# An LSH attention and token-mixing kernel on one core: idle-time matmuls at the start, new engines for the bit copies, and a new order of all steps

## The chip, the core and the metric

The kernel runs on one core of a Trainium2 chip. The core's engines work side by side, each through a queue of its own in program order: TensorE (PE, with its weight loads listed as PEld), VectorE (DVE), ScalarE (ACT), GpSimd (POOL) and SyncE (SP), which here issues nearly all DMAs. An engine waits at the head of its queue until semaphores of other engines or DMAs release it, and all that is queued behind waits too. The metric is the device time of one execution in microseconds (us); lower is better.

## The reference, cut to what matters

```python
batch, n_heads, seq, head_dim = 4, 8, 768, 64        # d_model 512, 6 projection bits
q_bits = (einsum('bhsd,dk->bhsk', q, proj) > 0)      # likewise k_bits
q_bucket = sum(q_bits * powers, axis=-1)             # likewise k_bucket
mask = q_bucket[:, :, :, None] == k_bucket[:, :, None, :]
scores = where(mask, matmul(q, k.T) / sqrt(64), -1e9)
attn = softmax(scores);  x = matmul(attn, v)         # heads side by side: (4, 768, 512)
theta = x @ w_theta
y = w_tok_r @ (x * cos(theta)) + w_tok_i @ (x * sin(theta))   # over the 768 tokens, per batch
u = x + y
out = u + maximum(u @ w_ch, 0)
```

## The kernel before, in words

Attention is done head by head in 16 pairs of heads (4 batches of 4 pairs; `prep_qk` and `prep_v` prepare a pair). Q and K are scaled by powers of two and split into a high and a low f16 half. The bucket test becomes part of the scores' matmul: the signs of the six projections of a pair are computed by `bits` (fp32 matmuls `pb`) and `sign` (DVE, L523, tile `rows`), and for each head its 24 rows of signs are copied below Q and K in the operand tile `qk` of that head. These copies are the operations `fbit` in `assemble`: four a head, each 24x384 f16, two for Q (a plain copy, on DVE or POOL at L588) and two for K (a multiplication by a column that is 1 in this head's rows and 0 in the others: on DVE or POOL at L586; on ACT both kinds stand at L584). The text calls the first plain copies and the second masking copies. There are three operand tiles, so a copy also waits until the last score matmul of the head that had the tile before. The first head of all has copies of its own (`piece`, lines 536 to 540).

A head then runs nine blocks of maxima (`qmax` on PE into tile `sq`, `vmax` on DVE, L632), which give a row bound that is written back into `qk` by a small DMA, then six or three score blocks per part (`st`), an exponential on ACT (`pf`, L713), its f16 rounding on ACT (`p1`, L719), the remainder on POOL (`p2`, L725) and the products with V on PE (`pv`, tile `po`). Ten heads of the later batches take another route (`bst`, `bmax` L836, `bpf` L864, `bp1` L872, `bp2` L878, `bpv`). When a batch's heads are done, `moe` runs the mixing for it: `proj` with w_theta (tile `ps_th`), sine and cosine, `zf`, `zh`, `zl` (L1109), 72 groups of three `y` matmuls (tile `py`), and `proj` with w_ch (tile `ps_r`), `relu`, `fin` and `store`. The weights are brought into f16 halves during the first batch (`wlow`, `whigh`, `wmul`, `wtl` on DVE, `wsign`, `wabs`, `wth` on ACT).

Nothing runs in the order in which it is written. The code first builds a list of 4263 operations. Each names one or more engines on which it may run with a planner's cost in ns, the operations it depends on and the buffers ("slots") that it holds. `issue_all` then issues them in the order of the string `ORDER`: each word is an engine letter (P, A, D, G for POOL, S) and the operation's number in base 36. The string `SLOTS` gives each slot the number of its buffer. Both strings were found by a search over the planner's costs outside the kernel; nothing of the search runs on the chip. PSUM has eight banks: two `mx`, two `s` and four `m`.

```python
own.append(op("fbit", prio + AB, {"POOL": (480, bits("POOL", i, x)), "DVE": (160, bits("DVE", i, x)),
                                  "ACT": (480, bits("ACT", i, x))}, t["bits"] + free_after, [sr]))
```

Of the kernel before, what the change touches and what calls it, by code (L numbers as in the profile page):

```python
# [32 lines left out]
def lsh_attention_moe_kernel(ctx: ExitStack, tc: tile.TileContext, q, k, v, proj, w_theta, w_tok_r, w_tok_i, w_ch, out):  # L33
# [6 lines left out]
    P = 128  # L40
# [524 lines left out]
    def assemble(j, n_, t, prio, free_after):  # L565
# [3 lines left out]
        sh, sr = t["slots"]  # L569
# [636 lines left out]
SETS = 3  # L1206
CL = 0.321
# [11 lines left out]
AB = 0.006  # L1219
# [47 lines left out]
    "0000000000000000000001010120112100212102100010000022001110100000011011011031022201000011221333111110000333122211110010310131201021"  # L1267
    "1001110310011130011111000200101101010210233013001322113302111000123303220111101030200110300130100013200002310011100013011110000100"
    "1120021011022213000211100011220311113312010121001100302011110320011110001100101301100100101111022312110300013313220011120013230132"
    "0001200120003110012000103000021010011100200110011100210311100020123211030311113213130201102000323130102201113101010320201131301201"  # L1270
    "1101200130000011010010011111110031131131232132003111032100302201131001212200010311221311120000321123020003111000000003210100001012"
    "0102320100123212131132001303320000102101031001201110010132101013231030110002221110330011310111111003103131000101130220023213200132"
    "0101031301101202111333103211110020100122012303100003000231010100110301301011213012012320223001003320301112311002301011111102002010"
    "3331031200002111110300013010111111012110231010113320010032311121231100003230112012011230101123310012000201111320200012100012001101"
    "0011201200111310323123101120000032300310112001013301030111013221102101032031111211110020010101011010012113230023101001323002301121"
    "2310100132300010223001230110331110103012012101200100010000121100001010201320101332010302111220101113030120003200111032100321012012"
    "0022301123030011310111300010111000011013102302120301201303023210111003022002321000032301020010113110232311003201322000010300001111"
    "0001111301211101031332002003031011012210030230101012000122321000131130220033110033101110330013211000101113100223101111220203103000"
    "1110111220003213113301013020122202001033013113100212000032112200321120001211211202212020200110110032200303112211020101310011320021"
    "1130002011320020201210021002311210002221120300123112020011001132002000221100113100301212012110211110030031010321012000022211110000"  # L1280
    "10112100021120000011021021012101021103200120001120000100120113002"
# [213 lines left out]
```

## Time and profile before

| | |
|---|---|
| time, median of 3 runs | 720.29 us (717.54 to 721.21) |
| the profiled execution | 716.42 us, of which the span from its first to its last instruction is 714.6 us |
| PE busy | 665.1 us (93% of the span) |
| ACT busy | 595.2 us (83%) |
| DVE busy | 586.0 us (82%) |
| POOL busy | 458.9 us (64%) |

The profile has one row a group of instructions: where it stands in the code, the tile written and read, the count, the busy time, the mean duration and the idle time of the engine just before it with what ended it. Matmuls are pipelined, so a mean duration of one holds the time in which it overlaps its neighbours; what a matmul costs in a stream is the distance from start to start. An fp32 matmul leaves two records.

### The profile page before, as it was taken

Reading aid. Unit: us, or ns where it says so; the run is one execution under the profiler, and the core shown is the slowest. Engines: PE = TensorE matmul, PEld = TensorE weight load, DVE = VectorE, ACT = ScalarE, POOL = GpSimd, SP = SyncE. Lnnn points to the kernel's source line nnn. Section 1 sums busy time; section 2 is a strip of 40 time slices with the busy share of each in tenths; the row PEclk is TensorE's granted clock in tenths of the full one; section 3 lists DMA queues with packets and bytes.
Section 4 is the critical chain, followed back from the end, with each engine's and each line's share of the span. In section 5 each row is a group of like instructions: output and inputs, shape, how many; then the busy total and the mean of one; then the engine's idle time right before and its main releaser. Section 6 shows DMA issues by size and latency. Waiting matters only on the chain.

```text
span 714.6 us, 16736 instructions
## 1 busy us (share of the span) xinstructions
PE 665.1 (93%) x6174; PEld 387.4 (54%) x6174; DVE 586.0 (82%) x1317; ACT 595.2 (83%) x1058; POOL 458.9 (64%) x448
## 2 busy tenths in 40 slices
PE   3788989989999999998999999999999999999997
PEld 1266657664555565555555566564545565654443
DVE  5899989999999899899998789878998766868221
ACT  6789989998999999999998898899898788876001
POOL 6566686868544787897847778886645878731011
PEclk9999999999999999999999999999999999999999
DMA  6748766666324557899864779797642866861112
GB/s 209 212 135 226 185 154 179 149 155 172 90 56 99 153 91 153 170 189 178 150 160 70 148 145 188 156 217 154 137 99 52 146 148 122 143 109 60 44 45 88
DMA packets 193304, 98.92 MB, mean 138 GB/s; under 512 B 166984, under 2 KB 182984, under 8 KB 193224
## 3 DMA queue, kind: packets, MB, share of 16 engines
q1 hardware_dynamic: 193080, 97.85, 62.2%
q8 instruction: 48, 0.79, 0.5%
q14 instruction: 32, 0.26, 0.1%
q10 hardware_dynamic: 144, 0.03, 0.0%
HBM read 32.53 MB, written 6.29 MB: 54 GB/s over the span
## 4 chain that ended last, share of the span: by engine, by line
PE 36%; DVE 18%; ACT 12%; issue 3%; ACTq 0%; DVEq 0%
PE py L77 16%; PE ps_r L77 6%; PE po L77 4%; PE st L77 3%; DVE bm L836 3%; ACT pf L864 3%; PE bt L77 3%; DVE mc L632 2%; PE ps_th L77 2%; PE sq L77 2%; ACT late L872 1%; ACT pf L713 1%; ACT p L719 1%; DVE f L1098 1%; DVE s_x L980 1%
## 5 line engine op out<-in xcount | busy, mean ns | idle before, releaser
L725 POOL TENSOR_TENSOR p<-pf,p 128x512 f16<-128x512 f32 x162 | 202.5, 1261 | 82.8 <-ACT p L719 60.1
L77 PE MATMUL py<-z,wtk 128*128 128x512 f16 x864 | 205.0, 379 | 1.2 <-DVE z L1109 0.8
L878 POOL TENSOR_TENSOR late<-pf,late 128x384 f16<-128x384 f32 x120 | 117.7, 993 | 52.4 <-ACT late L872 45.3
L77 PEld LDWEIGHTS <-qk 120*128 120x128 f16 (+2 forms) x1032 | 96.4, 101 | 96.8 <-issue 38.8
L632 DVE TENSOR_REDUCE mc<-sq 128x1 f32<-128x512 f32 (+1 forms) x198 | 131.1, 683 | 15.4 <-PE sq L77 14.2
L77 PEld LDWEIGHTS <-wtk 128*128 128x128 f16 x864 | 82.3, 98 | 94.4 <-issue 4.8
L713 ACT ACTIVATE pf<-st 128x512 f32<-128x512 f32 x198 | 114.4, 590 | 16.2 <-PE st L77 10.2
L77 PE MATMUL st<-qk 120*128 120x512 f16 (+3 forms) x528 | 116.8, 328 | 8.2 <-ACT pf L713 7.4
L719 ACT ACTIVATE p<-pf 128x512 f16<-128x512 f32 x162 | 99.5, 625 | 3.6 <-PE po L77 2.2
L77 PEld LDWEIGHTS <-p 128*128 128x128 f16 x1944 | 76.1, 97 | 23.7 <-POOL p L725 6.7
L77 PE MATMUL po<-vv,p 128*128 128x65 f16 (+1 forms) x1944 | 83.3, 193 | 5.4 <-POOL p L725 5.2
L77 PE MATMUL sq<-qk 120*128 120x256 f16 (+1 forms) x264 | 74.6, 338 | 14.7 <-DVE mc L632 7.2
L864 ACT ACTIVATE pf<-bt,bm 128x384 f32<-128x384 f32 x120 | 77.5, 665 | 12.6 <-DVE bm L852 8.2
L836 DVE TENSOR_REDUCE bm<-bt 128x1 f32<-128x384 f32 x120 | 63.4, 549 | 14.8 <-PE bt L77 13.0
L77 PE MATMUL ps_th<-wth,t_x 128*128 128x512 f16 x288 | 68.0, 379 | 0.3 <-DMA t_x<-s_x 0.3
L77 PE MATMUL ps_r<-wch,t_u 128*128 128x512 f16 x276 | 67.2, 379 | 0.6 <-DVE x L784 0.6
L872 ACT ACTIVATE late<-pf 128x384 f16<-128x384 f32 x120 | 60.5, 518 | 1.1
L77 PE MATMUL bt<-qk 120*128 120x384 f16 x240 | 55.3, 326 | 1.9 <-ACT pf L864 0.8
L1153 POOL TENSOR_TENSOR x<-rl,x 128x512 f32<-128x512 f32 x12 | 15.7, 1304 | 54.5 <-ACT rl L1150 54.5
L1150 ACT ACTIVATE rl<-ps_r,qu 128x512 f32<-128x512 f32 x23 | 15.6, 681 | 41.5 <-PE ps_r L77 41.5
L77 PEld LDWEIGHTS <-t_x 128*128 128x128 f16 x288 | 27.2, 98 | 29.5 <-DMA t_x<-s_x 1.1
L1137 DVE SCALAR_TENSOR_TENSOR x<-py,sw,x 128x512 f32<-128x512 f32 x24 | 17.9, 746 | 30.3 <-PE py L77 30.1
(180 smaller groups left out, 1147.4 us busy)
## 6 DMA issues: line engine op xcount, KB each, us to landing
qk<-hl SPq DMA_DIRECT2D x62, 192.0 KB
raw<-in_k_dram SPq DMA_DIRECT2D x16, 384.0 KB
raw<-in_q_dram SPq DMA_DIRECT2D x16, 384.0 KB
vb<-in_v_dram SPq DMA_DIRECT2D x16, 384.0 KB
out_dram<-x SPq DMA_DIRECT2D x24, 256.0 KB
qk<-hl SPq DMA_DIRECT2D x62, 96.0 KB
w_t<-in_moe_w_tok_r_dram SPq DMA_DIRECT2D x6, 768.0 KB
w_t<-in_moe_w_tok_i_dram SPq DMA_DIRECT2D x6, 768.0 KB
```

What stands on the lines that cost most here:

```text
L77: PE.matmul(out_, l, r, start=start, stop=stop, skip_group_check=True)
L632: DVE.tensor_reduce(col()[:, cs], u["sq"], AX.X, ALU.max)
L713: ACT.activation(wide("pf", spf, F32), u["st"], AF.Exp, scale=1.0 / (UNIT * math.sqrt(D)))
L719: ACT.activation(o_, u["pf"], AF.Copy)
L725: return lambda: eng.tensor_tensor(wide("p2", sp2, F16), u["pf"], u["p1"], ALU.subtract)
L836: DVE.tensor_reduce(part(y), w["w"], AX.X, ALU.max)
L864: ACT.activation(w["f"], w["w"], AF.Exp, bias=part(4), scale=part(3))
L872: ACT.activation(dst(0), w["f"], AF.Copy)
L878: return lambda: eng.tensor_tensor(dst(1), w["f"], dst(0), ALU.subtract)
L1137: DVE.scalar_tensor_tensor(tl[b][:, to], res["py"], t["sw"][:, to : to + 1], tl[b][:, to], ALU.mult, ALU.add)
L1150: ACT.activation(v_["r"], r_["ps"], AF.Relu, scale=t["qu"][:, to : to + 1])
L1153: return lambda: eng.tensor_tensor(tl[b][:, to], v_["r"], tl[b][:, to], ALU.add)
```

## The change

Three things change.

1. Twenty-four operations `spin` are added. Each is two fp32 matmuls of the 128x128 tile `ones` with itself into an `m` bank, and nothing reads what they write. They have no dependency except their bank. `ORDER` puts 22 of them among the first 148 operations: 8 stand ahead of PE's first operation (`bits` of the first pair), one after it, 5 after `qksum` and `vall` of the first pair, 5 among the nine maxima blocks of the first head, 3 among the maxima of the second head and the first score blocks. The other two are the 575th and the 879th operation of the order.
2. The planner's costs of the bit copies are set anew (a masking copy 1280 on POOL and 300 on DVE instead of 480 and 160; a plain one 540 on POOL instead of 480), and a masking copy is named `fmask`.
3. `SLOTS` and `ORDER` are new. Every operation is still there once. 162 operations have another engine. Of the 62 masking copies POOL had 28 and has 9, DVE had 14 and has 29, ACT had 20 and has 24; of the 62 plain copies POOL had 30 and has 33, DVE 15 and 11, ACT 17 and 18. Of 48 `zl` POOL had 9 and has 18, DVE 39 and 30; of 47 `xh` ACT had 29 and has 21, DVE 18 and 26; of 24 `fin` POOL had 12 and has 9; of 48 `zh` ACT had 34 and has 31; of 32 `qkh` ACT had 30 and has 28; of 24 `mag` ACT had 15 and has 17; of the two `fhi` of the first head ACT had both and DVE has one; of 18 `wmul` POOL had 9 and has 8. What these four lose or gain goes to or comes from DVE.

```diff
-                own.append(op("fbit", prio + AB, {"POOL": (480, bits("POOL", i, x)), "DVE": (160, bits("DVE", i, x)), "ACT": (480, bits("ACT", i, x))}, t["bits"] + free_after, [sr]))
+                own.append(op("fmask" if i else "fbit", prio + AB, {"POOL": (1280 if i else 540, bits("POOL", i, x)), "DVE": (300 if i else 160, bits("DVE", i, x)), "ACT": (480, bits("ACT", i, x))}, t["bits"] + free_after, [sr]))
...
+    for x in range(WARM):
+        def warm():
+            sw = Slot("m")
+
+            def spin():
+                w = bank(sw, [P, P], f"spin_{x}")
+                for _ in range(2):
+                    mm(w, ones, ones, True, True)
+
+            op("spin", QKL, on("PE", 432, spin), slots=[sw])
+
+        warm()
     issue_all()
...
+WARM = 24
...
 ORDER = """
-S5i S5g A0 D1 P5w A5j D5x A5h P5k D5l D5m S64 A65 G7g D5n D5o D5p P66 D5q A63 A60 D62 D5r S1q D67 D5u D5z A61 A5s D5v D5t D68 D69 D6a A5y
...
+P3ap P3ah P3ai S5i P3b1 P3b0 P3af P3au S5g P3ax A0 S64 A5j A5h D1 P5w D5x P3ar A60 A63 A65 P5k S1q D5l D5m D5n P66 D5o D5p D5q D5r D5z A5u
+D61 P3as A62 D5s A5y A76 D5v P3am P3aw A7g D67 Sa9 P3b2 G7d P3al P6i D68 A7b D5t A7a Sab S7c P6w D6j P3ay D69 D6a P3at A6b D6x P6s P6m D6t
...
```

(`P3af` to `P3b2` are the spins; `P5w` is the first pair's `bits`, `P5k` its `qksum`, `P66` its `vall`, `P6i` and `P6w` the first two blocks of maxima.)

## Rows read from the trace of the kernel before

**Rows 1.** Busy time by stage: PE, PEld, DVE, ACT, POOL; granted clock, DMA share, GB/s.

```profile
0.00:30.00 30.00, 14.72 (x49) 5.03 (x50) 21.61 (x55) 20.16 (x33) 14.99 (x37) 1.00 0.66 201
30.00:60.00 30.00, 25.80 (x266) 18.41 (x265) 28.97 (x54) 27.57 (x48) 18.96 (x19) 1.00 0.62 180
60.00:100.00 40.00, 33.33 (x341) 24.25 (x340) 35.23 (x70) 35.71 (x63) 31.82 (x26) 1.00 0.73 191
100.00:200.00 100.00, 91.94 (x886) 60.77 (x884) 94.07 (x195) 93.10 (x172) 69.80 (x59) 1.00 0.57 143
200.00:400.00 200.00, 195.19 (x1870) 110.30 (x1869) 182.60 (x430) 187.28 (x339) 145.56 (x136) 1.00 0.66 136
400.00:660.00 260.00, 254.00 (x2536) 145.56 (x2535) 210.53 (x498) 226.12 (x399) 172.71 (x169) 1.00 0.69 136
```

**Rows 2.** PE's groups by shape, 13 to 29.7 us: count, busy, mean ns, idle before.

```profile
L77 PE MATMUL sq<-qk 120*128 120x512 f16 x9 | 5.2, 599 | 7.1 <-ACT qk L536 4.9 <-DVE mc L632 2.2
```

**Rows 3.** The same group of PE, 29.8 to 60 us.

```profile
L77 PE MATMUL sq<-qk 120*128 120x512 f16 x14 | 5.1, 378 | 0.8 <-DVE mc L632 0.7
```

**Rows 4.** PE in order of time, 20 to 31 us: start, us, what.

```profile
25.16 0.85 PE L77 MATMUL pb<-raw,pst_q 128*32 128x384 f32 x1
...
28.11 2.34 PE L77 MATMUL st<-qk 120*128 120x512 f16 x6
30.29 0.38 PE L77 MATMUL sq<-qk 120*128 120x512 f16 x1
```

**Rows 5.** DVE and PE in order of time, the first 15 us.

```profile
0.86 0.17 DVE L63 MEMSET ones<- 128x128 f32 x1
...
5.65 0.82 PE L77 MATMUL pb<-raw,pst_q 128*32 128x384 f32 x1 [5.65 <-DMA raw<-in_q_dram]
...
7.33 0.68 DVE L523 TENSOR_SCALAR rows<-pb,pp 128x384 f16<-128x384 f32 x1 [2.88 <-PE pb L77]
...
9.12 1.12 DVE L540 TENSOR_SCALAR qk<-rows,pp 24x384 f16<-24x384 f16 x1
...
13.15 1.01 PE L77 MATMUL sq<-qk 120*128 120x512 f16 x2 [4.92 <-ACT qk L536]
```

**Rows 6.** PE in order of time, 703.5 to 705.2 us.

```profile
703.84 1.05 PE L77 MATMUL put<-diag,x 128*128 128x128 f32 x8
```

**Rows 7.** Who PE waited for, 30 to 200 us: total, times, longest.

```profile
PE po L77 <- POOL p L725: 4.1, 5, 2.7
PE pm L77 <- POOL vb L380: 1.4, 1, 1.4
```

**Rows 8.** Who ACT waited for, 30 to 200 us.

```profile
ACT pf L713 <- POOL p L725: 2.9, 4, 1.1
ACT n L1061 <- POOL wf_ch L229: 1.9, 1, 1.9
```

**Rows 9.** Who POOL waited for, 30 to 200 us.

```profile
POOL p L725 <- ACT p L719: 21.0, 11, 4.5
POOL qk L588 <- PE st L77: 7.2, 1, 7.2
```

**Rows 10.** POOL and PE in order of time, 86 to 100 us.

```profile
91.48 3.38 POOL L586 TENSOR_SCALAR qk<-rows,pp 24x384 f16<-24x384 f16 x2
...
99.43 0.48 PE L77 MATMUL po<-vv,p 128*128 128x65 f16 x10 [2.71 <-POOL p L725]
```

**Rows 11.** Groups by shape over the span: copies of rows, and the first `fhi`.

```profile
L586 POOL TENSOR_SCALAR qk<-rows,pp 24x384 f16<-24x384 f16 x28 | 38.6, 1379 | 5.5 <-issue 1.5 <-PE st L77 1.5
L588 POOL COPY qk<-rows 24x384 f16<-24x384 f16 x30 | 21.5, 716 | 12.0 <-PE st L77 7.2 <-DVE rows L523 3.2
L586 DVE TENSOR_SCALAR qk<-rows,pp 24x384 f16<-24x384 f16 x14 | 7.2, 513 | 0.4
L536 ACT ACTIVATE qk<-raw,sc 64x768 f16<-64x768 f32 x2 | 1.9, 928 | 1.3 <-DVE sc L502 1.3
```

**Rows 12.** The masking copies of L586 on DVE: ns min/median/max.

```profile
L586 DVE TENSOR_SCALAR qk<-rows,pp x14: 311/414/1197, 41.0 to 574.2; 24x384 f16<-24x384 f16 x14
```

More of the change, by code (lines that the diff above doesn't have):

```diff
@@ L1271 @@
[L1271 to L1278, printed above, removed]
@@ new lines @@
+    "1110110033122003011233010110200333011200312110012011310021110310011320001010111000100011011211100003211033021211000021133312000112"
+    "1321003001102130011000102000210011001101101111010110210221301000021203331121031002221133100111032022000320311122211030330132200111"
+    "1103100103000010111000111001011121022020102012012111002103303211210103202101010313210010033203231201103211101000130002210011001110"
+    "0000320322101011311323032102030032011001011002011130311032121103131010210101300111120011200111000100102230003202231310100100011010"
@@ new lines @@
+    "1123133201002333111332102111010000003323113212000101000321001011010201123111032001013011312123010010123001211011210013010002333111"
+    "2120131211100301110310012100001000002101122132110031330032212100331102301021101322110221300211111300010023201231110002000001101000"
+    "1001001123213100123120210311010030312210132010113111130221100230002301002110133020111000010210010011100111211111002031321123201100"
+    "2030121133201101303011221102013100332110020100121100020000200000110010300021201010123213031011110312320211132001122121112333003000"
@@ new lines @@
+    "1023020131110132031110320011200001100101100300010302211030122103120103103003211113012100012000221311332111210200003000010300013100"
+    "1000101101130011121012033000211130032112120303010322330131021010201013331113010102221110110011110100101011112112112201110030000310"
+    "2211131201001033013301102232001110030130103023013110000001112100011111000211111102102021003103210111010000012131110300220000311122"
+    "0030112000321120012120120201200023110010011300003112201121000032111011120000003111311220101012203002121110000013111230102210300001"
@@ new lines @@
+D7z P8u A8m Aas P80 G8n A8r Dbl D82 Pbc Dbd D81 S83 A8v Pbo A9a S84 Pat P8j A8w P8z Aew Dbp Sby Dau G8s D4 Pbg Pbq Dbr Pfb P8o Pbe Dbh Dav
+P9j Aey Pez Dbf Pbi Dbj A90 A5 Sh G8x A9b P9g A9h G97 Daw Df0 P8t Dc1 P8y Df1 Pbm Gc0 P9s Df2 Df3 Df4 Dax A91 Pba Df5 P9i Dbn A6 Df6 Dbb A9k
+D7 D8 A9t G9c G92 P93 Dbs Pbt Dc2 D9 P9p Dbv Gbz Pcj Da Aay Daz P9m Gb0 A9n Gb1 Sbx A9q Pc9 Dca Ad Dbu P98 P9l P9o Af7 Sbw Dck Dfc P9v P9y
+Ab Sf Df8 Af9 P9r De A9w A9z Pb2 P9u A1u Pc3 Di Pa4 Dfa Sfd Pcw Pcb Dcc Acx P9x Pa1 Ak Sjj Dj Sfr Aa2 Dc4 Pcf Gfu Pa0 Dcg Acy P9d Ab3 Db4
@@ new lines @@
+Gcz Pdb Pch Dci Al Adc Pc7 Dc8 Sjh Gfs Dm Pa3 Dc Aa5 Pcd Sg Add Dn Gft Gde Dce Pcr Acs Pc5 Dc6 Dcl Ajk Pa6 Pd6 Act Pd1 Ad2 Pcm Dfv Ad7 Dcn
+Da7 Do Afe Pg6 Ad3 Scp Pfy Sw Dfz Pdl Pdg Gcu Pcv Dco Scq Adh Pga Adm Pdv Pd0 Dp Pdq Gd4 Ad8 Gd9 Aji Dgb Pfw Dg7 Pgc Dfx Pd5 Pg2 Da8 Pff Dg3
+Adi As Gdj Dfg Pda Dt Ggm Pg0 Adn Dg1 Pjl D9e Dfh Gdo Adr Ago Adw Pe2 Ads Gdt D9f Djm Ggl Peb Pdf Dfi Dgd Pdk Djn Sgk Ae3 Pg8 Dg9 Djo Djp
+Djq Aq Su A1t Djr Djs Pdp Ggn Pe5 Ae6 Aec Pg4 Dfj Dg5 Pjx Ajt Afk Pe4 Dge Dr Pgf Pe8 Dx Sv Dgg Ae9 Pe7 Pgz Az Sgi Peh Pee Aef Pea D1v Aei
@@ new lines @@
+Adx Gdy Ped Pek Pgt Ael Dy D1w Dgh Dfl Gfm Gfn S1b Dju D1x Dh0 Sgj Peg Djy A10 Ph5 Phd Ahe Dh6 So5 Phi Dgu D11 Ahj Pgx Pej Ajv Pen Pfo D12
+Aeo Peq D13 D14 Gkf Afp Ph1 Pem Pep Ahk A17 Pdu Pdz Ahf Dh2 Ph3 Aer A15 Djw So3 D18 Akh Phn Aho Ghg Pih De0 Skd Sjz S19 Dfq Dh4 Aii Pgr Ahp
+Dkg Dgy Phh Pgv Ao6 Pi7 Ghl Dgs Phm Aij Pgp Dgw Ai8 D1c Dgq A1e Pes Gke Det Phs Dh7 Ph8 De1 Dh9 Gik Deu Aht Pkm Ao4 D1d Ahu Phx Pi2 Ghq Dha
+Po7 Do8 Shb Pko Dkn Ghv Ai3 Phr S2k D16 S1a Pkw Dkx Pic P3aj Phw Shc Dl9 Ahy Ahz Dkp Ai9 Do9 Doa Gl8 Poj A1f Dla Pky Pks D1g Gi0 Pir S3u Dkt
@@ new lines @@
+Dkz Aid Gl7 Pi1 Pio Gia Dob Doc Ak0 Pki Dkj Pkq Dkr Ai4 Sl6 Ais Gi5 D1h Aie Gif Pk1 Piu Aip Dk2 Pkk Pi6 Aiv Pix Dod Pj6 Pib D1i Dk3 Dk4 Dk5
+Piq Doe Ak6 D2l D2m Dk7 D1j Aj7 A2n Aiy S2q Pit Piw Pj0 Aoh Dkl A2o Gk8 Aj1 Doi Pku St7 Piz A1k Dkv A1m Gk9 Pj3 Aj4 Plf Dok Aof Dl0 Pj9 Aja
+Plr Dlg Pl1 Dl2 Sl4 Pj2 Pj5 Pld Pjc Dl3 G2p D2r D2s Pj8 A2t Plz Dog A2u G2v S2w Dls Ajd Pm4 Plp At8 Dle Gp0 Pka Am0 Pm9 Am1 St9 Am5 Sl5 D1y
+Akb Soz Dlq Pjb Am6 D1n Plb Dlc A21 Dkc Pje Plj Dlk Ama Gm7 Ap3 Pme Amf Plh Pmt Pig Dp2 Sol Amu Gp1 Dli Amb Pil Pll Gm2 Pmo S3o Dim Djf D2x
@@ new lines @@
+Ata Pmj Amk Pln Gmc Pm3 Pm8 Pmd Dlm Ppe Dlo D2y Dlt Amg Gmh Ppa Din Plu A2z Ptn Aml Dlv Dlw Amp Dpf Pmy Aom Pon Pmi Gmm Amq Slx Pn3 Dpb S32
+D1l Amz Sly Ppg Amv An4 A30 Pmn Ppi Djg Doo Gmr Pnd Ane Dph Dop Dpj Pp8 Sps Doq Gmw Ptb Dtc Png Pp4 Dpt S1p Pna Dor Pms An5 Aos Anb Dp9 Pp6
+S1o Pmx Dp5 Ppc G31 D33 Dot Pnc Dtd An0 Pnm A35 D34 Dte Apu Pnf Anh Dp7 A36 Gn6 Pnj Dtf Ppk Dtg Dpw Dth Apv Dpd Ank Pni Pqd Gn1 Dpl Pn2 Dto
+Pnp G37 Dti Dpm Ann D22 A1z Pns Ppn Gou Gov Pnl Pq5 D38 Atj Dpo S23 Anq Pnv D39 Ant Pny Spq Dtk Syb D3a Dq6 P3b D3c D3d Dpp Spr D3e Pno Pq1
@@ new lines @@
+Dv0 Psb Pre Prw Pum Dyi A2ku Asc P2kf P2kg Dud Dyj D2kv Gri Dyk Pua A2k7 D2k8 A3s Asd S2kw Grn Dun Grs A2k9 A2l4 Dub Ps1 As2 S25 Dyl Pui
+P2kn Dym Duj Pug Ps6 Prj Pro Duh Guy Ayn Arx A2kh Dyp P2ko D2l5 Prt Duz As3 As7 As8 Gs4 Ary D2ki D2jv P2kp P2kq Pue Puo Psg A2kr D2kj Dru
+Duf D2ks A2le P2kx Ash P2ky Dup S2l6 D2lf Gs9 Pv3 Pu8 Du9 Grz A2kt Ps0 Ps5 A2lo Dyo P2kz G3t Gse Pt0 At1 Psa Pvb Dv4 Duq Pur Psl Drv Asm Pu0
+Dus Suu Psf Pvd Au1 G3z P2l0 Dut D26 Asn D2lp D2lq D2lv Dve P2l7 P2l8 S2lg P2l9 P2la G2lr D2ly A2l1 Psq Du2 A2lz Asi Asr D2l2 Psv A2lw Pyr
@@ new lines @@
+D2ls A2lt D2m0 D27 Gso P2lh Pv1 Dv2 P2li A2lb Pvu Avv P2lj P2lk D2lc Ass G2lu Pvp Dvc Pvf Gst A29 D2lx P2o0 Syt At2 P2o1 Pv7 P2o2 Gsj Dvg
+Dyq Asw Pv9 A2ll A2ld Avq Gt3 D2lm Dys S40 Pwe Psk Psp Asx Gsy Psu Avw Pwj P2nd P2ne Dva Awf D2ju Pvh P2nf Sz7 D2m4 Az8 Awk D2m1 Psz Awg
+P2mq Dz9 Pw9 S143 Gwh P2mr A2l3 Dv8 A2m5 Avr D2ln D2m2 Gvs Azb P2ng Pvz Dvi Pv5 Dza Pzg Pt4 Dv6 Dvj G2m3 Dt5 A2m7 G2m6 D41 A43 P2ms Suv Dzh
+Pzk P2o3 P2nh S141 Dt6 P2mt Pvk Pzo D42 A44 Awa D2mb D2m8 D2m9 D2mc P2mu P2mv Gvx D2ma D2md D45 Dvl D2me A28 P2o4 P2ni Pw4 Aw5 Aw6 Svn P2mw
@@ new lines @@
+P2o5 D2mn Dzp Dvm Gw7 Aw0 Ayu A2mf G2mg A2mo D2js D2mh P2o6 Pwo P2o7 Pyv A2mi P2nj A142 S46 A144 Dyw Dyx Dyy Dyz Awp P2mx D2mj Az0 D2a D2b
+S4i Pzs Pvt Pvy Aw1 Dzl D2c G2mp D2d A2e P2nk D2mk A2ml Px5 Dzt Gw2 P2my Ax6 P2nl P2nm Pzm Awb P2mz Pwt A104 D2mm A2g Gwc Awu P2o8 D2f Pw3
+Awl P2o9 Pw8 D47 S100 P2oa P2n0 Dz1 D48 D103 Pzi A49 P2nn Px0 P2no D4j D4k Pwd A4l Dzn Pze Awq Gwr P2n1 D2jt A4a Pwi D2np P2ob A4m Svo Dzj
+D2n2 Pxa Ax7 Gwm Pwn D2h P145 P2pa S4c S2i Awv A102 G4n S4u Gww D2jw Pws S2j Pzq D146 D4b Gx8 Dzr Ax1 Pxf Axb D4d P2pb Axc Gxd Dzf D147 D148
@@ new lines @@
+A106 G11p Py3 A4r D2nr P2pl A12k G127 S14x A12h D4z P2oq D2n4 S2n5 A12i A12l P2or D4t S2ns D50 G12j D51 Py8 A14k D52 G12m Dy9 P10a A10b P154
+A10c P15a Dya D15b P2os P53 P14l G11s P10k P10z A107 S11t A10l S19r D155 G108 P152 D54 P2ot D55 P156 A110 P2ou D56 A10m P10f D57 A5e D2pm
+D14m G10n D157 P119 D14n A5c P2ov D5f A10g P15g A5a P2ow P10p A11a D153 P15i G10d D15h D5d A10q A10h P109 D5b P2ox P114 D15j P2oy A58 P158
+D14o A19u G10i A115 D59 A19s D14p P10e P15c P12p P10j A111 A2od D159 D2oz P10o P10u D2p0 G15s A10r S15q P12r P2n6 A14q P2nt D15d A11b S128
@@ L1427 @@
+P385 P386 D387 P372 G33q P373 P39x P37p P37q D388 P37r P395 P374 P396 P39y P39z P397 P398 A37s P399 P39a P39b D38v D38w D37t S37u P39c D389
+S38x D3a5 P38y P38z P390 P39d P39e P39f P39g P391 S38a P38b A392 P3a0 D39h D39i D39j P3a1 P3a2 P3a3 P38c A375 S33r D3a4 P38d G393 P38e P3a6
+S39k D376 S394 P39l P39m A38f G38g S38h S377 A3a7 D3a8 P39n P39o A39p G39q S39r P3a9 P3aa P3ab A3ac D3ad S3ae
 """
```

255 lines of the change are left out of this document (106 added, 149 removed).

## The prediction, made before the changed kernel was run

> **What bounds the kernel now.** I read the busy time by stage first [rows 1]. From 200 us to 660 us PE is busy 449.2 of 460 us: there PE sets the pace, and what other engines do costs time only where it leaves PE idle. Before 200 us it is otherwise. PE is busy 165.8 of 200 us, so 34.2 us of its idle time, most of all there is, lie in this part. From 30 to 200 us DVE is busy 158.3 of 170 us and ACT 156.4: these two set the pace, with PE close behind and POOL at 80% in the stretch from 60 to 100 us. So the change has to be judged by what it does before 200 us.
>
> Then the first 30 us, for the clock. The column of the granted clock reads 1.00 there, but the matmuls speak against it: a 512-column matmul of the maxima takes 599 ns before 29.7 us and 378 ns after [rows 2, 3], and six 512-column matmuls from 28.11 us take 2.34 us, which is the low level, 1.2 GHz (512 columns in some 0.43 us) [rows 4]. At 30.29 us the same kind takes 0.38 us, the high level. The rise lies between, after PE had worked closely from 25.16 us on; from 13 to 25 us it had worked with pauses and stayed low. So 14.72 us of PE work run at half speed, and at the high level about 7.4 us of that would go.
>
> Last the waits. From 30 to 200 us PE waits 4.1 + 1.4 = 5.5 us for POOL [rows 7] and ACT 2.9 + 1.9 = 4.8 us [rows 8]. One such wait can be seen whole: two masking copies hold POOL from 91.48 us for 3.38 us, the remainder tile behind them comes late, and PE stands for 2.71 us until 99.43 us [rows 10]. POOL pays 1379 ns for a masking copy, DVE 513 [rows 11].
>
> **The change part by part**, in time added (+) or won (-).
>
> *The eight spins ahead of the first `bits`.* No row shows this matmul; the nearest is four fp32 matmuls of 128x128 by 128 columns at the high level, eight records in 1.05 us, 0.13 us a record at most [rows 6]. I take 0.11 (the last one's overhang taken off, my choice), so 0.44 us a spin of four records, and 0.88 at the low level. They need `ones`, written at 0.86 + 0.17 = 1.03 us [rows 5]. `bits` could start at 5.65 us. If the clock never rose, the eight would end at 1.03 + 8 x 0.88 = 8.1 us, 2.4 us late. The one rise that the trace shows came between 28.11 and 30.29 us, PE having worked closely from 25.16 us [rows 4]; let the spins' own rise come likewise, at 5.6 us (my choice, between the two ends below): 5.2 spins low, 2.8 high, end at 6.9 us, 1.2 us late. Then `bits` takes half: the 1.7 us from its start to the sign's start at 7.33 us become about 0.9. Net +0.4. Ends: -0.9 (high from the start) and +2.4.
>
> *The new start on DVE.* The copy of L540 (1.12 us, from 9.12 us) stood between two steps of the scale chain and now stands behind it; one `fhi` comes to DVE, nearest price 0.93 us from ACT [rows 11]. That frees PE's first maxima block earlier than 13.15 us, but the first `vmax` has nearly the same work before it in DVE's queue: +0.2, between -1.1 and +0.9.
>
> *The later spins.* Twenty stand where PE waits for DVE or DMA; PE has 15.3 us idle in the first 30 [rows 1]. Two stand after that, 0.9 us together where PE has 6.7 us idle in 40: +0.2, at most 0.9.
>
> *The high level until 30 us.* It takes up to 7.4 us from PE, but from 30 to 60 us DVE is busy 28.97 of 30: work that PE does sooner waits for DVE. Only what DVE itself waits for PE is won. I take -1.0, ends 0 and -7.4; the 97% of DVE speak for the small one.
>
> *POOL rid of masking copies.* Counted in the two orders, POOL's queue ahead of the last `p2` of the first batch holds 3 masking copies instead of 13 and 14 plain ones instead of 11: 10 x 1.379 - 3 x 0.716 = 11.6 us less [rows 11]. The waits of PE and ACT for POOL lie in the same stretch, 10.3 us together [rows 7, 8]. I take 10/13 of PE's 5.5, which is 4.2, and a quarter of ACT's 4.8, since its waits overlap PE's in part: -5.4. Ends: 0 (other waits take their place) and -10.3.
>
> *DVE gets them.* Ahead of the last `vmax` of that batch DVE has 8 masking copies instead of 1, and the `fhi` (one plain copy fewer and one reciprocal more left aside): 7 x 0.513 + 0.93 = 4.5 us [rows 11]. DVE is idle 11.7 us from 30 to 200 us [rows 1], so part is covered; I charge half, +2.2. Ends: 0, and 7 x 1.197 + 0.93 = 9.3 at the longest copy seen [rows 12]. ACT's side: three masking copies more, fewer of other kinds; nothing, since ACT's idle 13.6 us there covers it, and at worst 1.9.
>
> *The rest of the new order.* After 200 us PE has 10.8 us idle in 460 and each stage keeps its work; POOL loses nine more masking copies: -0.5, between -2 and +2. The tail is PE alone and doesn't change.
>
> Sum: 0.4 + 0.2 + 0.2 - 1.0 - 5.4 + 2.2 - 0.5 = -3.9 us. The profiled execution took 716.42 us (span 714.6, 1.8 us around it), 3.9 us less than the median of 720.29; the sum is a difference, so it goes on the median: 720.3 - 3.9 = 716.4 us, 0.54% less. A run of this kernel tells 0.5% (3.6 us) from nothing.
>
> **The rivals.**
>
> *POOL's waits come back as waits for others.* POOL itself waits 21.0 us for ACT's rounding in this part [rows 9], so a `p2` that no longer stands behind a masking copy often stands behind `p1`. Then POOL's term is worth some -1.5 instead of -5.4, and the sum is 0: 720 us. Against it: the 2.71 us wait above hangs on the copies alone.
>
> *The clock doesn't do what it is held for.* If it rises late, or falls while PE waits for the second pair's loads, the start costs +2.4 and the high level gives 0: -3.9 + 2.0 + 1.0 = -0.9, 719.4 us. For it: from 13 to 25 us PE was busy with pauses and stayed low. Against it: the spins stand in those pauses.
>
> *Slower: DVE becomes the bound.* A masking copy on DVE while POOL works can take 1197 ns, and POOL is busy 80% from 60 to 100 us [rows 1, 12]. If most do, DVE's term is the 9.3, and with everything behind it in the queue waiting, half of POOL's gain is gone: -3.9 + 7.1 + 2.7 = +5.9, 726.2 us. It decides once DVE's added time passes POOL's gain by some 5 us. For it: DVE is busy 97% from 30 to 60 us, and the copies also wait for the last score matmul of a former head, which once held POOL 7.2 us [rows 9]. Against it: the median of fourteen is 414 ns. The Trainium skill, SBUF — State Buffer, section Who interferes with whom, says that a DVE copy in its two-port mode and a GpSimd instruction exclude each other for the whole instruction, the later one standing still. By that rule the long copies would be the common ones; the median [rows 12] says that most went free.
>
> *Much faster.* A third of PE's 34.2 us idle before 200 us goes, as order and clock help each other: -11, 709 us.
>
> **How the numbers follow.** Forecast (-3.9 with its spread of some 2 us) 0.36, much faster 0.10, POOL's waits come back 0.22, clock without effect 0.13, slower 0.19. The forecast lies close to the bound of 0.5%, at 716.7 us, so I count two thirds of it as faster and let the rest fall to the same; of the two middle rivals a tenth of a chance, where the new order helps elsewhere, goes to faster. Faster 0.36 x 2/3 + 0.10 + 0.10 = 0.44, same 0.12 + 0.25 = 0.37, slower 0.19. The range goes from the much faster case, 708, up past the middle ones to 724, which leaves out most of the slower case and little below: 708 to 724. The forecast's own is 714 to 719.
>
> **What would show it.** In the profile after: 512-column matmuls at 378 ns well before 29.7 us, and the first `bits` within 2 us of 5.65; DVE's first `vmax` within 1 us of before; PE's waits for POOL from 30 to 200 us down from 5.5 to some 1.5 us; DVE's masking copies near 0.5 us each; PE's idle time before 200 us down from 34 to about 30 us, with the spins counted as idle. I am wrong if these copies average over 0.9 us, if PE's idle time moves to waits for ACT or DVE, or if the time after 200 us changes by more than 2 us.

## The result and the profile after

The changed kernel takes 726.73 us (median; 721.57 to 728.09) beside 720.88 us of the kernel before on the same chip (715.09 to 724.51): ratio 1.0078, interval 1.0054 to 1.0102. It is slower by more than the 0.5% bound and lies above the forecast of 716.4 us and its range. The profiled execution after took 727.22 us (span 725.4, mean granted clock 0.975), that of before 716.42 us (span 714.6, clock 0.998), one of the quicker ones of its kernel; the medians are 5.9 us apart, the two profiles 10.8.

**The stages** (busy time of the kernel after; PE, PEld, DVE, ACT, POOL; granted clock, DMA share, GB/s), against [rows 1]:

```profile
0.00:30.00 30.00, 22.79 (x133) 17.28 (x134) 20.58 (x56) 19.39 (x32) 13.10 (x36) 0.90 0.62 205
30.00:60.00 30.00, 25.44 (x235) 17.88 (x234) 24.35 (x50) 24.43 (x44) 18.19 (x14) 0.90 0.55 159
60.00:100.00 40.00, 38.92 (x332) 28.81 (x332) 33.81 (x68) 34.32 (x60) 21.25 (x21) 0.81 0.59 164
100.00:200.00 100.00, 89.82 (x883) 60.75 (x883) 95.52 (x199) 90.57 (x167) 61.99 (x56) 0.97 0.66 152
```

POOL is relieved as meant: 21.25 us busy instead of 31.82 from 60 to 100 us. But the clock column, 1.00 throughout before, falls to 0.81 there, PE's busy time rises from 33.33 to 38.92 us though it does no more work, and DVE and ACT, which set the pace before, are less busy from 30 to 100 us. PE busy for longer is here PE at half speed. The same can be read off one kind of matmul, the 512-column maxima (count, busy, mean ns; stretches 7.2 to 24.2, 24.2 to 31.1, 31.1 to 55 and 55 to 75.4 us), against 599 and 378 ns in [rows 2, 3]:

```profile
L77 PE MATMUL sq<-qk 120*128 120x512 f16 x6 | 2.1, 379 | 0.4 <-DVE mc L632 0.4
...
L77 PE MATMUL sq<-qk 120*128 120x512 f16 x4 | 2.3, 621 | 0.8 <-DVE mc L632 0.8
...
L77 PE MATMUL sq<-qk 120*128 120x512 f16 x9 | 3.4, 379 | 0.1
...
L77 PE MATMUL sq<-qk 120*128 120x512 f16 x6 | 3.8, 632 | 0.0
```

The spins did bring the high level early, at 7.2 us. It was lost at 24.2 us, won again at 31.1, and lost once more at 55 us for 20.4 us (and for 3.4 us each near 110 and 151 us). Busy time and clock around these falls, columns as above:

```profile
24.20:31.10 6.90, 6.12 (x22) 3.50 (x22) 6.27 (x12) 3.66 (x7) 1.41 (x2) 0.51 0.34 97
31.10:51.00 19.90, 18.72 (x209) 13.21 (x207) 19.52 (x45) 19.90 (x37) 14.59 (x14) 1.00 0.55 170
51.00:55.00 4.00, 0.62 (x6) 0.28 (x5) 3.28 (x4) 2.88 (x5) 3.60 (x1) 1.00 0.63 102
55.00:75.40 20.40, 20.40 (x91) 14.87 (x91) 10.45 (x20) 10.80 (x20) 5.99 (x6) 0.50 0.42 106
```

In the four microseconds ahead of 55 us PE is busy for 0.62; then it is busy for all of 20.40 us at 0.50, 1.2 GHz, while DVE and ACT stand half of the time. What stopped PE is seen in order of time (start, us, what; in brackets the idle time before and its releaser), 49 to 62 us:

```profile
49.92 4.68 POOL L380 TENSOR_TENSOR vb<-vb 128x128 f32<-128x128 f32 x2
...
50.62 1.00 DVE L473 SCALAR_TENSOR_TENSOR hl<-raw,sc,hl 128x768 f16<-128x768 f32 x1
...
51.55 0.94 DVE L301 TENSOR_TENSOR wf_t<-wf_t 128x768 f16<-128x768 f32 x1
...
53.28 1.00 DVE L473 SCALAR_TENSOR_TENSOR hl<-raw,sc,hl 128x768 f16<-128x768 f32 x1
...
54.65 0.41 PE L77 MATMUL pm<-vb,ones 128*33 128x128 f32 x2 [3.38 <-POOL vb L380]
...
59.19 0.60 ACT L713 ACTIVATE pf<-st 128x512 f32<-128x512 f32 x1 [5.31 <-PE st L77]
...
59.56 0.69 DVE L632 TENSOR_REDUCE mc<-sq 128x1 f32<-128x512 f32 x1 [5.27 <-PE sq L77]
```

`vmean` of the second pair needs the sums that `va2` makes on POOL. The two adds of `va2` took 0.99 us in the kernel before (from 49.65 us); here they take 4.68, the second alone 4.15 against 0.46. Beside it DVE runs its own operations without a pause from 50.0 to 54.3 us, and POOL's add ends at 54.6. DVE was no less busy beside the adds before (4.94 of 5 us from 45 to 50, 5.00 from 50 to 55); what is new is which of its operations stand there: three of the five have two inputs in SBUF. PE stands for 3.38 us, with scores and maxima behind `vmean` in its queue; ACT and DVE, which want these, then stand for 5.3 us each. The Trainium skill, SBUF — State Buffer, section Who interferes with whom, says that a DVE instruction with two inputs in SBUF contends with a GpSimd instruction that reads SBUF, and calls the contention an exclusive lock. The trace agrees as far as it goes: 4.15 us beside such instructions of DVE (the three in the rows) and two with one input, 0.46 us in the kernel before, where the add had begun beside a reduction. No run here moved these DVE operations away.

Waits from 30 to 200 us (total, times, longest), against [rows 7 to 9]:

```profile
POOL p L725 <- ACT p L719: 32.2, 16, 10.4
ACT pf L713 <- PE st L77: 18.6, 14, 5.3
DVE mc L632 <- PE sq L77: 8.8, 6, 5.3
...
PE sq L77 <- DVE mc L632: 6.2, 11, 1.4
...
PE pm L77 <- POOL vb L380: 3.4, 1, 3.4
```

PE's wait for POOL's remainder tiles, 4.1 us before, is gone. ACT's wait for PE's scores was 6.5 us before and is 18.6: PE at half speed is what is late now.

The start (order of time), against [rows 5]:

```profile
1.08 6.73 PE L77 MATMUL spin<-ones 128*128 128x128 f32 x32 [1.08 <-DVE ones L63]
...
7.74 0.51 PE L77 MATMUL pb<-raw,pst_q 128*32 128x384 f32 x1
...
8.66 0.68 DVE L523 TENSOR_SCALAR rows<-pb,pp 128x384 f16<-128x384 f32 x1 [4.65 <-PE pb L77]
...
14.52 0.69 DVE L632 TENSOR_REDUCE mc<-sq 128x1 f32<-128x512 f32 x1
```

And the masking copies over the span (busy, mean ns), against [rows 11]:

```profile
L586 DVE TENSOR_SCALAR qk<-rows,pp 24x384 f16<-24x384 f16 x29 | 17.5, 602 | 0.9
...
L586 POOL TENSOR_SCALAR qk<-rows,pp 24x384 f16<-24x384 f16 x9 | 11.8, 1308 | 7.8 <-PE st L77 7.1
```

### The profile page after: what moved, and what is told of

Read it like the earlier page. It is cut to its first block, busy times and chain, and to the rows that moved or that the text cites. A ratio compares the mean times of both kernels' runs of the same rounds, so it can differ in the third digit from the quotient of the medians.

```text
span 725.4 us, 16920 instructions
## 1 busy us (share of the span) xinstructions
PE 684.5 (94%) x6270; PEld 408.3 (56%) x6270; DVE 603.5 (83%) x1334; ACT 592.3 (82%) x1052; POOL 445.0 (61%) x437
## 4 chain that ended last, share of the span: by engine, by line
PE 54%; DVE 27%; ACT 10%; issue 5%; DMA 2%; POOL 1%; SPq 0%; ACTq 0%; DVEq 0%
PE py L77 18%; PE po L77 11%; PE st L77 6%; DVE mc L632 6%; PE ps_r L77 6%; PE bt L77 4%; PE sq L77 4%; DVE s_x L980 2%; DVE bm L836 2%; DVE hl L473 2%; ACT pf L864 2%; ACT pf L713 2%; PE ps_th L77 1%; DVE f L1098 1%; DMA vb<-in_v_dram 1%
## 5 line engine op out<-in xcount | busy, mean ns | idle before, releaser
L725 POOL TENSOR_TENSOR p<-pf,p 128x512 f16<-128x512 f32 x162 | 200.0, 1246 | 94.4 <-ACT p L719 74.1
L77 PE MATMUL py<-z,wtk 128*128 128x512 f16 x864 | 207.4, 379 | 2.8 <-ACT z L1103 1.3
L878 POOL TENSOR_TENSOR late<-pf,late 128x384 f16<-128x384 f32 x120 | 121.7, 1025 | 53.6 <-ACT late L872 48.4
L77 PE MATMUL st<-qk 120*128 120x512 f16 (+3 forms) x528 | 121.2, 339 | 5.5 <-ACT pf L713 3.3
L77 PE MATMUL sq<-qk 120*128 120x256 f16 (+1 forms) x264 | 76.3, 341 | 10.8 <-DVE mc L632 9.5
L1109 POOL TENSOR_TENSOR z<-f,z 128x512 f16<-128x512 f32 x18 | 25.8, 1442 | 43.9 <-ACT z L1103 24.3
L77 PEld LDWEIGHTS <-late 128*128 128x128 f16 x1080 | 39.0, 97 | 9.0 <-issue 1.6
```

Of the source, the lines that this page charges most:

```text
L77: PE.matmul(out_, l, r, start=start, stop=stop, skip_group_check=True)
L725: return lambda: eng.tensor_tensor(wide("p2", sp2, F16), u["pf"], u["p1"], ALU.subtract)
L878: return lambda: eng.tensor_tensor(dst(1), w["f"], dst(0), ALU.subtract)
L1109: return lambda: eng.tensor_tensor(t["z"][r, 1][:, tt], u["f"], t["z"][r, 0][:, tt], ALU.subtract)
```

## The experiments

The theories: **C**, PE's idle time ahead of `vmean` lets the clock fall, and the low level behind it costs the time; **S**, the spins cost it themselves, by the early rise or by their place in PE's queue; **D**, the masking copies on DVE cost it (my slower rival). Microseconds are medians of all executions. Ratios are to the kernel before beside it in the same session, and are not those of the medians: e1's median is 719.14 us against 720.77, which is 0.9977, but its ratio is 1.0011, since a few of its executions are long. Where a ratio and a median disagree, the interval decides.

| run | what it is | us | ratio (interval) |
|---|---|---|---|
| e1_no_spin | after, no spins | 719.14 | 1.0011 (0.9981 to 1.0040) |
| e2_vmean_later | after, `vmean` later | 715.98 | 0.9945 (0.9914 to 0.9975) |
| e3_hold | after, 8 spins more ahead of `vmean` | 718.03 | 0.9982 (0.9951 to 1.0013) |
| e4_before_spin | before, with 24 spins | 719.60 | 0.9986 (0.9963 to 1.0009) |
| f1_later_no_spin | e2 without spins | 714.25 | 0.9921 (0.9891 to 0.9952) |
| f2_later_old_masks | e2, old engines of masks | 732.26 | 1.0154 (1.0119 to 1.0189) |
| f3_before_vmean_early | before, `vmean` early | 723.83 | 1.0036 (1.0006 to 1.0066) |
| f4_before_early_hold | f3 with 10 spins | 727.94 | 1.0096 (1.0065 to 1.0126) |
| g1_first_eight | after, first 8 spins only | 720.83 | 1.0007 (0.9968 to 1.0046) |
| g2_later_sixteen | after, later 16 only | 723.14 | 1.0041 (1.0012 to 1.0070) |
| g3_before_new_masks | before, new engines of masks | 727.97 | 1.0085 (1.0056 to 1.0113) |
| g4_later_five_spins | f1 with 5 spins at the start | 716.65 | 0.9944 (0.9917 to 0.9971) |
| h1_hold_alone | e1 with 5 spins ahead of `vmean` | 716.59 | 0.9952 (0.9927 to 0.9977) |
| h2_before_early_three | f3 with 3 spins | 722.26 | 1.0009 (0.9986 to 1.0031) |
| h3_later_only_sixteen | f1 with the later 16 spins | 715.89 | 0.9931 (0.9909 to 0.9953) |

**Spins, `vmean`'s place, a hold.** e1 leaves the 24 spins out. e2 moves two operations of the order behind a score block:

```diff
-P9r De A9w A9z Pb2 P9u A1u Pc3 Di Pa4 Dfa Sfd Pcw Pcb Dcc Acx P9x Pa1 Ak
+P9r De A9w A9z P9u A1u Pc3 Di Pa4 Dfa Pcw Pcb Dcc Acx P9x Pa1 Pb2 Sfd Ak
```

(A part of a line of `ORDER`. `Pb2` is the `vmean` of the second pair, now behind seven more operations of PE, where the expectation below says eight; `Sfd` is a load of V that reuses its buffer.) e3 puts eight more spins right ahead of `Pb2`, where PE waits. e4 keeps the order of before and adds 24 spins at the corresponding places.

```diff
-WARM = 24
+WARM = 0
```

(that line, and the spins' entries in `ORDER` and `SLOTS`, for e1; 32 for e3.)

> The changed kernel with its 24 spins taken out; order, banks and engines of all else as changed. Theory C (the changed kernel lost its time to falls of the clock, above all 20.5 us at the low level from 55 us, behind a 3.4 us wait of vmean for POOL, and that wait belongs to the new order): the first 30 us are at the low level as in the kernel before, the wait of vmean stays, and the fall with it; 724 to 728 us. Rival S (the spins themselves bring the falls, by raising the clock while PE is still working with pauses): the clock rises once near 30 us and stays; 720 to 722 us. Rival D (the masking copies moved to DVE cost the time, whatever the clock does): 726 to 728 us with no fall needed.

> The changed kernel with the mean of the second pair's V (vmean) issued eight PE operations later, and the load that reuses its buffer behind it; nothing else moved. Theory C: PE no longer stands 3.4 us for POOL near 51 us, the clock doesn't fall at 55 us, and 20.5 us at the low level go: 718 to 722 us. Rival S: other falls take its place, 724 to 727. Rival D: 726 to 728, the wait was covered by DVE.

> The changed kernel with eight spins more, right ahead of that vmean, so that PE works through the 3.4 us in which it waits for POOL; the wait itself stays, since the spins' 3.5 us fill it. Theory C: the clock holds at 55 us and the time falls to 718 to 723 us though PE has more to do. Rival D: 727 to 730, the 3.5 us of spins come on top where they outlast the wait. If e2 gains and this doesn't, the wait and not the clock was the price.

> The kernel before with 24 spins in its own order, at the places among PE's operations that answer to those of the changed kernel; engines and order of all else as before. My prediction's reckoning: some 1 us more at the start, 1 us back from the high level, so 720 to 721 us. Rival S: the clock rises early and then falls in PE's pauses between 15 and 60 us, and the time is 722 to 726. Theory C says nothing beyond: without a wait of several us on PE the clock holds, 719 to 721.

Moving one `vmean`, a single fp32 matmul, brings 10.8 us back (726.73 to 715.98), and eight spins that fill the wait bring 8.7; in e3's trace the level holds from 33 us until past 600. The loss hangs on that idle time, as C says. But leaving the spins out brings 7.6 as well (4.8 by the ratios, 1.0078 less 1.0011), where C expected 724 to 728 us: C alone doesn't explain it, and S, with 720 to 722, came nearer. In the order of before the same number of spins changes nothing that can be told (0.9986). So neither the spins nor the wait does it alone. In the profile of e1 the wait is there (3.4 us) and the clock falls behind it, for 6.8 us instead of 20.4:

```profile
49.00:53.50 4.50, 2.21 (x19) 1.79 (x18) 4.50 (x8) 4.50 (x6) 4.34 (x3) 1.00 0.41 77
53.50:60.30 6.80, 5.71 (x23) 4.13 (x23) 1.30 (x2) 1.26 (x4) 1.03 (x1) 0.50 0.38 124
60.30:75.40 15.10, 12.60 (x138) 9.35 (x138) 14.70 (x25) 13.84 (x27) 10.67 (x10) 1.00 0.64 166
```

**Both out; the masks back.** f1 is e2's order without any spin. f2 is e2 with 41 of the 62 masking copies on the engines that the kernel before gives them (only the engine letters in `ORDER` differ; 23 go back to POOL, 4 leave it).

> The changed kernel with vmean of the second pair eight PE operations later (as in e2) and with all 24 spins taken out. If the spins earn what they were added for, it is slower than e2 (716.0 us) by what the high level is worth in the first 30 us: 717 to 720. My prediction put that at 1 us or less: 716 to 717. If the spins do harm by an early rise that is lost again (rival S, fed by e1, where taking them out won 7 us): 712 to 715.

> e2 with the 62 masking copies back on the engines that they had before (28 on POOL, 14 on DVE, 20 on ACT), at the places of the new order; spins kept. Rival D (masking copies on DVE cost time): faster than e2, 711 to 714 us. My prediction (POOL's relief is worth 5.4 us and DVE's load costs 2.2): slower than e2, 718 to 721. If the copies' engine matters little: 715 to 718.

f1 is the best kernel here, in the bounds that S set: 0.9921 of the kernel before, 0.9828 of the kernel after (714.25 / 726.73). f2 loses 16.3 us against e2, so D falls for the new order: there the copies on DVE cost less than they give. With 28 of them back on POOL, PE and ACT wait for its remainder tiles again (30 to 200 us):

```profile
PE po L77 <- POOL p L725: 5.3, 6, 1.8
ACT pf L713 <- POOL p L725: 3.7, 4, 1.9
```

**The wait carried into the kernel before.** f3 takes before's order and puts `va1`, `va2` and `vmean` of the second pair earlier, so that PE waits; f4 adds ten spins ahead of it, h2 three. (A part of a line; the three words go where they stood, further on.)

```diff
-Aay A6 A9k Daz Pch Dck
+Aay A6 A9k Daz Gb0 Gb1 Pb2 Pch Dck
```

> The kernel before with the second pair's va1, va2 and vmean issued earlier, right behind vv2, so that PE stands some 4 us for POOL there; nothing else changed. Theory C: the wait by itself costs little, since DVE and ACT have work, but the clock falls behind it in most runs: 723 to 728 us and a lower granted clock than the kernel before. Rival (the price is the wait): 3 to 4 us more, 724, with the clock as before. If neither matters there: 720 to 722.

> As f3, with ten spins (4.4 us of PE work at the high level) right ahead of that vmean, so that PE works through the wait. Theory C: the clock holds there and the time goes back to 719 to 722 us though PE does more. Rival (the price is the wait): as f3 or slower.

> The kernel before with va1, va2 and vmean of the second pair early (723.8 us, TensorE idle for 2.4 us ahead of vmean) and with three spins in that idle time: 3 x 0.75 = 2.3 us. The earlier try with ten took 7.5 us, three times what there was to fill. Theory C: the fall at 49.5 us goes and the time comes back to 721 to 722.5 us. Theory W: 723.5 to 724.5 us.

f3 loses 2.5 us against the kernel before beside it (723.83 against 721.29): PE waits 2.39 us for the sums, and the clock falls for 3.4 us behind it (columns as above).

```profile
45.00:49.50 4.50, 1.99 (x24) 0.96 (x22) 3.02 (x15) 3.21 (x5) 2.52 (x4) 1.00 0.58 238
49.50:52.90 3.40, 3.40 (x32) 2.48 (x30) 3.16 (x3) 1.48 (x3) 0.48 (x1) 0.50 0.44 121
```

f4 was misdosed. Its ten spins ran 7.53 us where 2.4 were to be filled, and `vmean` began at 54.12 instead of 48.93 us; a delay of 5.2 us, enough for the 4.1 that f4 takes beyond f3. Theory C's expectation was missed; in f4's trace the clock does hold there (the first fall is at 103.8 us), but its time tells nothing on what a fall costs. With three spins (2.15 us) the fall is gone,

```profile
45.00:49.50 4.50, 3.93 (x39) 2.83 (x38) 3.66 (x16) 3.86 (x7) 2.36 (x5) 1.00 0.71 291
49.50:52.90 3.40, 3.32 (x41) 2.50 (x42) 2.55 (x3) 1.91 (x3) 1.14 (x2) 1.00 0.34 97
```

and 722.26 us is where C put it, but the intervals of f3 and h2 overlap, so in time this pair does not decide. Nor do the two traces: other falls come after 100 us in both, 13.7 us low in all in each, and the two executions took 722.58 and 722.26 us.

**Which spins; the masks alone; a short start.**

> The kernel after with only the eight spins at its start; the sixteen later ones are left out. The kernel after measured 726.7 us with all 24 spins and 719.1 with none, so 7.6 us lie in the spins. Theory F (the first eight do it: with them bits starts at 7.74 instead of 5.36 us, and TensorE stands at its high level from 7 us on, when the later stages still leave it idle, so that it falls early and often): 725 to 727 us. Theory L (the later sixteen do it: they stand in TensorE's queue ahead of matmuls for which others wait, up to 158 us): 719 to 721 us, bits still at 7.74. If both count, the time lies between, near 723.

> The kernel after without its first eight spins; the sixteen later ones stay. Theory F: 719 to 721 us, with bits at 5.4 us and the clock low until 25 us or later. Theory L: 725 to 727 us. If both count, near 723. If the two parts need each other (the first raise the level, the later ones let it fall), both this run and its twin stay near 720.

> The kernel before, in its own order and without spins, with 41 of the 62 masking copies on the engines that the kernel after gives them (10 go from POOL to ACT, 13 from POOL to DVE, 8 from ACT to DVE, 6 from DVE to ACT, 4 from ACT to POOL). Theory A (what the choice of engines is worth stands by itself: going back to the old choice cost 16.3 us in the order with vmean later, 732.3 against 716.0): 703 to 709 us. Theory B (engines and order were chosen together, and each is worth something only with the other): 716 to 724 us, with new waits of TensorE for p where a copy now stands behind another operation on DVE or ACT. My forecast's term for it was a gain of 3.2 us (5.4 less 2.2), which would give 717.5.

> The kernel after with vmean of the second pair later and with five spins, all at the start; the other nineteen are left out. Five spins end near 1.1 + 5 x 0.84 = 5.3 us, when the load for bits has landed, so that nothing is late. The same kernel without spins measured 714.25 us, with all 24 spins 715.98. If a level raised early is worth the 1.0 us that my forecast gave it: 713.0 to 713.6. If spins ahead of a stage that leaves TensorE idle bring falls: 715 to 716.5. If the five are too few to raise the level: 714 to 714.5, with the 512-column sq matmuls at 0.6 us until 25 us or later.

By their medians g1 and g2 lie 1.7 and 4.0 us above e1, all 24 lie 7.6 above; but each interval alone overlaps e1's, and g1's ratio (1.0007) is not above e1's (1.0011). That the first eight cost time by themselves is not shown. g3 is the clear miss of both my sum and Theory A: the new engines in the old order cost 6.5 us more, where the sum's two terms said 3.2 less. Engines and order are worth something only together (Theory B). In g4 the five spins raise the level at 4.4 us and lose it again at 11.3 (the same columns):

```profile
4.40:11.30 6.90, 2.46 (x19) 1.49 (x17) 4.62 (x12) 5.82 (x11) 6.74 (x10) 1.00 0.76 291
11.30:31.80 20.50, 15.10 (x45) 4.89 (x46) 18.65 (x39) 14.69 (x26) 5.44 (x7) 0.50 0.68 182
```

It gains nothing over f1 (716.65 against 714.25).

**The wait or the fall behind it.** h1 has no spins but five ahead of `vmean`; h3 has `vmean` later and the sixteen later spins.

```diff
-P9r De A9w A9z Pb2
+P9r De A9w A9z P3af P3ag P3ah P3ai P3aj Pb2
```

> The kernel after without its 24 spins, but with five spins right ahead of the vmean that waits 3.4 us for POOL (5 x 0.75 = 3.75 us at the high level). Without any spin it measured 719.1 us; with vmean later and without any spin 714.25. Theory C (of these 4.9 us the fall of the clock behind the wait is a part, and the wait itself the rest): the low stretch of 6.8 us at 53.5 us goes, and the time is 716 to 717.5 us. Theory W (the wait alone costs it, since ACT and DVE stand behind it; the fall is without price): 719 to 720 us, whether the clock falls or not.

> The kernel after with vmean of the second pair later and with the sixteen later spins alone. Without spins it measured 714.25 us, with all 24 it measured 715.98, with five at the start 716.65. With vmean early the sixteen cost 4.0 us (723.1 against 719.1). Theory P (each spin has its price in TensorE's queue, wherever vmean stands): 717.5 to 718.5 us. Theory G (the spins cost what they do only through falls behind the idle time of vmean): 714 to 715.5 us.

h1 takes 716.59 us, inside Theory C's bounds. In its profile PE runs spins, waits for the rest, and keeps the high level where e1 fell:

```profile
50.59 2.45 PE L77 MATMUL spin<-ones 128*128 128x128 f32 x20
54.13 0.41 PE L77 MATMUL pm<-vb,ones 128*33 128x128 f32 x2 [1.09 <-POOL vb L380]
```

```profile
53.50:60.30 6.80, 6.17 (x56) 4.96 (x57) 3.63 (x5) 3.53 (x7) 2.87 (x2) 1.00 0.47 140
```

The spins do no work for the kernel, `vmean` is hardly earlier (54.13 us, 54.59 in e1), and still 2.5 of the 4.9 us between e1 and f1 come back. The trace splits it alike: the 41st matmul of the maxima starts at 52.7 us in f1, 56.5 in h1 and 59.1 in e1, so the wait costs 3.8 us and the fall behind it 2.6, less up to 0.5 for the earlier `vmean`. One thing speaks for caution: among e1's own executions the time does not go with small differences of the clock (718.7 to 720.1 us at a mean clock of 0.995, 718.9 to 719.3 at 0.998), and only one trace of each kernel was kept. h3 lies 1.6 us above f1, between its two theories and with intervals that overlap: where no wait is, sixteen spins cost little or nothing.

## Why the prediction was wrong

**The clock was entered as a gain only.** The step that failed is *The high level until 30 us*, taken at -1.0 with ends 0 and -7.4. The rise came (379 ns from 7.2 us on, well before 29.7), but I gave no price to a fall after it. My rival on the clock named a fall, "while PE waits for the second pair's loads", and priced it at the gains that would be missing, 719.4 us. The falls from 55 us on lie in the stretch that [rows 1 to 3] show at the high level all through, so they lose what the kernel before had. Between the profiles of e1 and after, the same matmul of the maxima starts level at 59.1 and 58.9 us; the 61st is 4.2 us later (83.6 against 87.8), the 121st 7.3 (166.1 against 173.4), the last `py` 7.3 (705.3 against 712.6). After 31 us the kernel after is low for 27.3 us, e1 for 10.2: 7.3 / 17.1 = 0.43 us lost for each us at the low level. So in this pair most of what the spins cost goes with the clock. It is not all of it: the trace of g2, with the sixteen later spins, is low after 31 us for only 6.8 us against e1's 10.2, and still its last `py` is 2.8 us later than e1's (708.1 against 705.3). So spins also cost by their own place in the queue.

**The wait that replaced the old one.** *POOL rid of masking copies* at -5.4: the waits named did go (4.1 to 0 for PE, 2.9 to 0 for ACT's `pf`). What I left out is `va2`. [rows 7] showed `vmean` waiting 1.4 us for it, and I counted its wait among those that would shrink; it grew to 3.4, because POOL's second add, beside other operations of DVE than before, took 4.15 us. I had weighed a lock between DVE and POOL, but only for the masking copies on DVE; what was held, if the lock is the cause, was another operation, on POOL. My slower rival named 726.2 us, half a microsecond from what was measured, but that is luck: it wanted copies of up to 1197 ns on DVE, and they averaged 602.

**The sum of terms.** Without spins and with `vmean` later (f1) the new engines and order gain 6.6 us (720.88 to 714.25), more than the 3.5 that the terms without the clock and the spins make (0.2 - 5.4 + 2.2 - 0.5). That direction was right, though g3 and f2 show that it can't be split as I split it, and no run shows the -5.4 and the +2.2 as they stand: the same copies cost 6.5 us on their new engines in the old order and 16.3 on the old engines in the new one. The chain of the whole is then: -6.6 engines and order, +4.9 `vmean` ahead of its data (of which some 2.5 are the clock), +7.6 the spins on top: +5.9. These are medians; by the ratios the three links are some -5.7, +6.5 and +4.8, so each is known to 2 or 3 us.

**The small steps.** Eight spins ended at 7.81 us, within the ends, and `bits` started 2.09 us late, just past the 2 us that I allowed; half the time of its matmuls made up for part, and the first `vmax` came at 14.52 us instead of 14.22, so the start's +0.4 and +0.2 hold. A spin took 0.49 us in h1 (2.45 / 5) against my 0.44. DVE's masking copies took 602 ns, not 513, still under the bound of 0.9. PE's idle time before 200 us, spins counted as idle, is 39.9 us (200 less 176.97 busy, plus 16.88 of spins) where I said 30 and [rows 1] give 34.2. After 200 us little changes, as I said: the first `py` is 9.0 us later than before (202.8 against 193.8), the last 10.9.

**What stays open.** Why the fall lasts 20.4 us in the kernel after and 6.8 in e1, behind the same wait, the runs don't show; the spins of the kernel after are spent by then, but for two far behind. The long fall does not need the later spins: the trace of g1, with the first eight alone, shows one of 13.7 us from 54.5 us. That execution took 726.32 us where the median of g1 is 720.83, so the fall seems not to come in each. Why POOL's add is held is argued from the trace alone. Nor is it settled how the 7.6 us divide between the first eight and the later sixteen.

## What to carry to other kernels

A clock held high by work without use is worth only what the stages behind it can take, and it can be lost again at the first place where TensorE stands still: before adding such work, list the long waits of TensorE (2.4 and 3.4 us here) in the stages that already run at the high level, and move their cause. Price a wait of TensorE as the wait and the half-speed stretch that may follow it (here 3.8 and some 2 to 2.6 us). When an order is searched anew, look at the short operations on GpSimd that feed TensorE directly: beside other operations of VectorE one took nine times as long.

## What the runs showed of the hardware

The low level held through 20.40 us in which the profile shows TensorE without a pause (after, 55 to 75.4 us), and through 13.70 us in e2; I had taken close work to be enough for a rise, as at 25 to 30 us in the kernel before:

```profile
135.00:139.10 4.10, 2.77 (x30) 2.21 (x30) 4.00 (x10) 3.66 (x8) 2.64 (x3) 1.00 0.74 152
139.10:152.80 13.70, 13.70 (x68) 10.64 (x65) 9.91 (x24) 7.66 (x13) 0.51 (x2) 0.50 0.44 94
```

Ahead of three falls TensorE had stood for one long wait: it was busy for 0.62 of 4.00 us (after), 2.21 of 4.50 (e1), 1.99 of 4.50 (f3). The fall of e2 had no such wait ahead of it: TensorE was busy for 2.77 of 4.10 us, and its longest wait there was 1.1 us.

The time of one and the same kernel goes with the clock granted over its execution. Over 105 executions of the kernel before, taken beside the experiments, the correlation of the time with the share of the clock lost is 0.91: 715 to 719 us at a mean clock of 0.996 and above, 722 to 726 at 0.987 and below. That is more than this change was forecast to bring.

The price of a spin seems to hang on its bank (no run varied it alone). The three of h2 and the ten of f4, which all write one bank, took 0.72 and 0.75 us each (2.15 / 3, 7.53 / 10); the five of h1 and the eight of e3 ahead of `vmean`, which take turns on two, 0.49 and 0.47 (2.45 / 5, 3.79 / 8).
